# Row-shaped products with 512 moving weight columns, and a result stored in two halves

## Chip, cores and metric

The kernel runs on one core of one Trainium2 chip. The metric is the device time of one execution in microseconds (us). Before the change three runs took 415.16, 415.17 and 415.35 us, median 415.17. The profile is of one more execution.

## What is computed

One decode step for one token: a normalised row times wq gives 32 query heads; grouped attention over 4 key and value heads with 65,536 positions each; output projection; then a feed-forward block with gelu. x has 1024 elements, everything is bf16.

```
x  = A_x                                   # 1 x 1024
q  = layernorm(x) @ wq                     # 1024 x 4096, 32 heads of 128
o  = softmax(q k^T / sqrt(128)) v          # per group: 8 heads share 65536 x 128 of k and v
h  = x + o @ wo                            # 4096 x 1024
n  = layernorm(h)
h2 = h + (gelu(n @ w_gate) * (n @ w_up)) @ w_down    # 1024 x 3584, 1024 x 3584, 3584 x 1024
```

## The kernel before, in words

All weights and both caches are read once from HBM, 173 MB in all. SP issues every load, in program order, as transfers of up to 4 MB into one pool of four buffers (`chpool`): two for wq, 32 for K and V, two each for wo, gate, up and down. A load waits for the engine that still reads its buffer, and for one of eight completion semaphores: the ninth load after another waits for that one's landing. Each load has one packet for each of the 128 partitions, and they are spread evenly over 16 DMA engines.

Vectors of the token live as columns. Element `p * 8 + c` of x or h lies in partition `p`, column `c` (`x_col`, `h_col`); a matrix row with the same number is loaded to the same place (`"(p c) n -> p c n"`). LN1 and LN2 (`layernorm_cols`, L126) make `xn_bf` and `hn_bf` of them.

- q (L156 to L163): for each of 8 row groups `c` and 32 heads, a 128 x 128 block of wq is the stationary operand, and one column of `xn_bf` moves through it. The heads' 32 columns add up in `q_ps`.
- qsel and qs (L164 to L178): q is spread by selectors, then copied by POOL into zeroed tiles `qs`, one per group of heads (32 copies early on, 16 for each of two groups).
- K (L198): DVE transposes 128 x 1024 tiles into `kt` (a pool of six), PE multiplies with `qs`, DVE transposes scores back (L225) and takes maxima. The V pass of a group (L255) runs beside the K pass of the next one.
- wo (L297 to L335): `o2z` holds each of 32 columns of the attention result in a zeroed block of 32 columns, so that a product with 512 moving columns of wo writes 32 partitions, one of which is the result. Four column groups of the array (`tile_position`) take the 32 matrix rows in turn, `s` picks one of two PSUM banks. The four partial sums of each bank are copied out (L328 on DVE, L330 on ACT), and eight fp32 matmuls against a column of ones sum and turn them into columns, `hc_ps` (L333).
- Gate and up (`ffn_in`, L343): like q, but with 28 blocks per row group, whose columns are 28 apart (`f:F:FC`): 224 products each. Gate is loaded in two pieces, up in four (4, 2, 1 and 1 row groups). The gelu of gate is worked out in DVE and ACT beside up's products.
- Down (L380 to L398): 28 row groups with 8 blocks each (columns 8 apart), again one moving column, loaded in pieces of 10, 6, 4, 3, 2, 1, 1 and 1 row groups; the last of them goes in three parts of 8, 8 and 112 partitions.
- The residual is added at L402, and SP stores 16 bytes from each partition at L403.

The order on each engine is the program's, but for small pieces of work that the scheduler may move ahead.

Of the kernel before, what the change touches and what calls it, by code (L numbers as in the profile page):

```python
# [17 lines left out]
def kernel(  # L18
# [13 lines left out]
    nc = tc.nc  # L32
# [18 lines left out]
    DCH = 2  # L51
    CW = DCH * CH * Dh
    assert NCH % DCH == 0
    scale = float(Dh) ** -0.5
    eps = 1e-5
    assert Dh == P and rep * NS == SQ and NT % (CH * NH) == 0 and D % P == 0 and F % P == 0
# [69 lines left out]
    def layernorm_cols(src_col, dst_bf, tagp):  # L126
        s1 = small.tile([P, 1], F32, name=f"{tagp}_s1", tag="ln_s1")
        nc.vector.tensor_reduce(out=s1[:], in_=src_col, axis=AX.X, op=ALU.add)
        tot = misc([P, 1], F32, f"{tagp}_tot")
        nc.tensor.matmul(tot[:], lhsT=ones_f[:], rhs=s1[:], start=True, stop=True)  # L130
        mean = small.tile([P, 1], F32, name=f"{tagp}_mean", tag="ln_mean")
        nc.vector.tensor_scalar(out=mean[:], in0=tot[:], scalar1=1.0 / D, scalar2=None, op0=ALU.mult)
        xc = small.tile([P, DC], F32, name=f"{tagp}_xc", tag="ln_xc")
        nc.vector.tensor_scalar(out=xc[:], in0=src_col, scalar1=mean[:, 0:1], scalar2=None, op0=ALU.subtract)
        sq = small.tile([P, DC], F32, name=f"{tagp}_sq", tag="ln_sq")
        s2 = small.tile([P, 1], F32, name=f"{tagp}_s2", tag="ln_s2")
        nc.vector.tensor_tensor(out=sq[:], in0=xc[:], in1=xc[:], op=ALU.mult)
# [7 lines left out]
        nc.vector.tensor_scalar(out=dst_bf, in0=xc[:], scalar1=rstd[:, 0:1], scalar2=None, op0=ALU.mult)  # L145
# [168 lines left out]
    NW = D // 512  # L314
    at_ps = [misc([P, 512], F32, "at_ps") for _ in range(NW)]
    for w0 in range(0, Hq, WN):
        w_sb = chunk("wo_sb")
        wv = w_sb[:, 0:WN * D].rearrange("p (c n) -> p c n", c=WN)
        nc.sync.dma_start(out=wv, in_=wo_v[:, w0:w0 + WN, :])
        for cc in range(WN):  # L320
            c = w0 + cc
            q = c % 4
            for s in range(NW):
                nc.tensor.matmul(at_ps[s][32 * q:32 * q + 32, :], lhsT=o2z[:, c, :],  # L324
                                 rhs=wv[:, cc, s * 512:(s + 1) * 512],
                                 start=(c < 4), stop=(c >= Hq - 4), tile_position=(0, 32 * q))
    at_r = ktpool.tile([P, D], F32, name="at_r", tag="kt")
    nc.vector.tensor_copy(out=at_r[:, 0:512], in_=at_ps[0][:])  # L328
    for s in range(1, NW):
        nc.scalar.copy(out=at_r[:, s * 512:(s + 1) * 512], in_=at_ps[s][:])  # L330
# [7 lines left out]
    hn_bf = const.tile([P, DC], BF16, name="hn_bf")  # L338
    layernorm_cols(h_col[:], hn_bf[:], "ln2")
    GB = max(1, CW // F)  # L340
    assert DC % GB == 0

    def ffn_in(wmat, name, pieces):  # L343
        ps = misc([P, FC], F32, name)
        nc.vector.memset(ps[:], 0.0)
        wv_all = wmat.rearrange("(p c) n -> p c n", p=P)
        assert sum(pieces) == DC
        for c0 in range(0, DC, GB):
            w_sb = chunk("wgu_sb")
            wv = w_sb[:, 0:GB * F].rearrange("p (c n) -> p c n", c=GB)  # L350
            r0 = 0
            while r0 < GB:
                sz = pieces.pop(0)
                nc.sync.dma_start(out=wv[:, r0:r0 + sz, :], in_=wv_all[:, c0 + r0:c0 + r0 + sz, :])
                for cc in range(r0, r0 + sz):
                    for f in range(FC):
                        nc.tensor.matmul(ps[:, f:f + 1], lhsT=wv[:, cc, f:F:FC], rhs=hn_bf[:, c0 + cc:c0 + cc + 1],  # L357
                                         start=False, stop=False, skip_group_check=True)
# [17 lines left out]
    act_bf = const.tile([P, FC], BF16, name="act_bf")  # L376
    nc.vector.tensor_tensor(out=act_bf[:], in0=u_ps[:], in1=gl[:], op=ALU.mult)  # L377


    wd_v = B_w_down.rearrange("(p c) n -> p c n", p=P)  # L380
    DN = CW // D
    pieces = [[10, 6], [4, 3, 2, 1, 1, 1]]
    assert sum(map(sum, pieces)) == FC and max(map(sum, pieces)) <= DN
    d_ps = misc([P, DC], F32, "d_ps")
    nc.vector.memset(d_ps[:], 0.0)
    c0 = 0
    for group in pieces:
        w_sb = chunk("wd_sb")
        r0 = 0
        for sz in group:  # L390
            wv = w_sb[:, r0 * D:(r0 + sz) * D].rearrange("p (c n) -> p c n", c=sz)
            last = c0 + sz == FC
            for lo, hi in ((0, 8), (8, 16), (16, P)) if last else ((0, P),):
                nc.sync.dma_start(out=wv[lo:hi], in_=wd_v[lo:hi, c0:c0 + sz, :])
            for cc in range(sz):
                for j in range(DC):
                    nc.tensor.matmul(d_ps[:, j:j + 1], lhsT=wv[:, cc, j:D:DC], rhs=act_bf[:, c0 + cc:c0 + cc + 1],  # L397
                                     start=False, stop=False, skip_group_check=True)  # L398
# [3 lines left out]
    nc.vector.tensor_tensor(out=h2[:], in0=d_ps[:], in1=h_col[:], op=ALU.add)  # L402
    nc.sync.dma_start(out=out[0, 0].rearrange("(p c) -> p c", p=P), in_=h2[:])  # L403


# [28 lines left out]
```

## Time and profile before

| | us |
|---|---|
| the profiled execution | 414.91 |
| its span, first to last instruction | 413.1 |
| median of three other runs | 415.17 |
| PE busy (matmuls) | 256.8 |
| DVE busy | 201.9 |
| ACT busy | 35.9 |
| POOL busy | 27.1 |
| bytes moved | 173.33 MB, 420 GB/s over the span |
| q products, L160 (256) | 7.2 |
| gate products, L357 (224) | 14.3 |
| up products, L357 (224) | 14.3 |
| down products, L397 (224) | 13.6 |
| wo products, L324 (64) | 6.9 |
| fold of wo's result, L333 (16 passes) | 3.9 |

PE is the tensor engine's matmuls and PEld its weight loads, which overlap; DVE, ACT and POOL are the vector, scalar and general engines; SP issues DMAs. The page's slices cut the span in 40 equal parts, and each digit is the busy share in tenths; PEclk is the tensor clock as granted. In a timeline, a line has the start, the length, engine, line of the kernel, operation, tiles, shapes and count, and in brackets how long the engine idled and for whom. An "xN" after a busy time is a number of instructions. An fp32 matmul shows as two passes.

### The profile page before, as it was taken

To read this page: it belongs to the slowest core of one execution; us is meant where nothing else is said; L and a number is where in the kernel's file an instruction comes from. 1 tells how busy PE (TensorE), PEld (TensorE's weight loads), DVE (VectorE), ACT (ScalarE), POOL (GpSimd) and SP (SyncE) were. 2 spreads that over 40 slices of the span, in tenths; PEclk is the share of its full clock that TensorE was granted. 3 is DMA by queue.
4 is the path that set the end of the run, shared out by engine and by line. 5 is a ranking of instruction groups with operands and counts; after the bars stand their busy time and mean duration, and the time that the engine had idled before them with its cause. 6 is when DMAs were issued, how large, how long until landed. Compare 5 with 4: busy or idle time off the path is not lost.

```text
span 413.1 us, 4925 instructions
## 1 busy us (share of the span) xinstructions
PE 256.8 (62%) x2117; PEld 138.3 (33%) x2117; DVE 201.9 (49%) x254; ACT 35.9 (9%) x135; POOL 27.1 (7%) x100
## 2 busy tenths in 40 slices
PE   1336677698291838765566388191928335479997
PEld 1332222243130314221222233030314113279997
DVE  3107999999393808856474389291910000010000
ACT  1000000070000080000003400000071000000000
POOL 8123000310000210000000000000000000000000
PEclk9999989989886867895959698777796755655555
DMA  8999999999999999999999999999999999999993
GB/s 356 420 439 432 428 435 424 431 431 427 435 428 435 427 432 428 430 431 431 424 435 428 435 428 433 428 435 427 431 431 427 435 428 436 423 431 414 425 409 115
DMA packets 7413, 173.33 MB, mean 420 GB/s; under 512 B 992, under 2 KB 992, under 8 KB 1888
## 3 DMA queue, kind: packets, MB, share of 16 engines
q1 hardware_dynamic: 7360, 173.02, 98.0%
q8 instruction: 16, 0.26, 0.3%
q14 instruction: 5, 0.04, 0.0%
q10 hardware_dynamic: 32, 0.00, 0.0%
HBM read 173.02 MB, written 0.00 MB: 419 GB/s over the span
## 4 chain that ended last, share of the span: by engine, by line
DMA 52%; DVE 23%; PE 15%; issue 9%; SPq 0%; POOLq 0%; ACT 0%; POOL 0%; ACTq 0%
DMA k_sb<-in_A_k_cache_dram 44%; DVE kt L211 19%; DMA v_sb<-in_A_v_cache_dram 8%; PE g_ps L357 3%; PE u_ps L357 3%; PE d_ps L397 3%; PE qk_ps L215 2%; DVE mx L226 2%; DVE sc L225 2%; PE acc_ps L264 1%; PE o_ps L278 0%; SPq L87 0%; POOLq L429 0%; ACT acc_sb L275 0%; PE mxT_ps L233 0%
## 5 line engine op out<-in xcount | busy, mean ns | idle before, releaser
L215 PE MATMUL qk_ps<-kt,qs 128*128 128x512 bf16 x512 | 143.7, 436 | 78.8 <-DVE kt L211 76.7
L211 DVE STREAM_TRANSPOSE kt<-k_sb 128x1024 f32<-128x1024 f32 x128 | 146.2, 1208 | 53.5 <-DMA k_sb<-in_A_k_cache_dram 53.5
L215 PEld LDWEIGHTS <-qs 128*128 128x128 bf16 x512 | 54.9, 107 | 164.5 <-issue 120.9
L248 ACT ACTIVATE pt<-sc,nbias 128x256 bf16<-128x256 f32 x64 | 31.5, 492 | 275.2 <-DVE nbias L241 275.2
L264 PE MATMUL acc_ps<-v_sb,pt 128*32 128x512 bf16 x512 | 38.0, 444 | 13.5 <-DMA v_sb<-in_A_v_cache_dram 13.5
L357 PEld LDWEIGHTS <-wgu_sb 128*128 128x128 bf16 x448 | 28.5, 172 | 1.3 <-issue 1.3
L280 DVE TENSOR_TENSOR oT_all<-o_ps,rl 128x8 bf16<-128x8 f32 x4 | 0.7, 167 | 55.1 <-PE o_ps L278 55.1
L264 PEld LDWEIGHTS <-pt 128*32 128x32 bf16 x512 | 13.9, 107 | 33.0 <-issue 25.2
L225 DVE STREAM_TRANSPOSE sc<-qk_ps 128x512 f32<-128x512 f32 x32 | 22.1, 692 | 2.1 <-PE qk_ps L215 2.1
L226 DVE TENSOR_REDUCE mx<-sc 128x8 f32<-128x512 f32 x32 | 22.0, 688 | 1.1
L278 PE MATMUL o_ps<-sel,acc_sb 128*128 128x8 f32 x32 | 7.5, 364 | 21.8 <-ACT acc_sb L275 21.8
L357 PE MATMUL g_ps<-hn_bf,wgu_sb 128*128 128x1 bf16 x224 | 14.3, 202 | 1.2 <-DVE hn_bf L145 1.2
L278 PEld LDWEIGHTS o_ps<-sel,acc_sb 128*128 128x128 f32 x32 | 7.1, 328 | 23.0 <-ACT acc_sb L275 23.0
L357 PE MATMUL u_ps<-hn_bf,wgu_sb 128*128 128x1 bf16 x224 | 14.3, 202 | 0.0
L173 POOL MEMSET qs<- 128x2048 bf16 x4 | 7.2, 1803 | 102.6 <-PE qk_ps L215 102.6
L160 PE MATMUL q_ps<-xn_bf,wq_sb 128*128 128x1 bf16 x256 | 7.2, 165 | 10.8 <-DMA wq_sb<-in_A_wq_dram 10.8
L397 PE MATMUL d_ps<-act_bf,wd_sb 128*128 128x1 bf16 x224 | 13.6, 198 | 0.3 <-DVE act_bf L377 0.3
L397 PEld LDWEIGHTS <-wd_sb 128*128 128x128 bf16 x224 | 13.6, 164 | 0.2 <-issue 0.2
L177 POOL COPY qs<-qsel 32x32 bf16<-32x32 bf16 x64 | 11.2, 247 | 17.1 <-DVE qsel L168 16.4
L324 PE MATMUL at_ps<-wo_sb,o2z 128*32 128x512 bf16 x64 | 6.9, 609 | 8.5 <-DMA wo_sb<-in_A_wo_dram 8.5
L248 ACT ACTIVATION_READ_ACCUMULATOR pt<-sc,nbias 128x1 f32 x64 | 11.9, 186 | 0.0
L312 POOL MEMSET o2z<- 128x1024 bf16 x1 | 0.9, 950 | 156.6 <-PE acc_ps L264 156.6
(80 smaller groups left out, 61.3 us busy)
## 6 DMA issues: line engine op xcount, KB each, us to landing
k_sb<-in_A_k_cache_dram SPq DMA_DIRECT2D x16, 4096.0 KB, 29.8
v_sb<-in_A_v_cache_dram SPq DMA_DIRECT2D x16, 4096.0 KB, 33.1
wq_sb<-in_A_wq_dram SPq DMA_DIRECT2D x2, 4096.0 KB, 12.1
wo_sb<-in_A_wo_dram SPq DMA_DIRECT2D x2, 4096.0 KB, 36.5
wgu_sb<-in_B_w_gate_dram SPq DMA_DIRECT2D x2, 3584.0 KB, 33.4
wgu_sb<-in_B_w_up_dram SPq DMA_DIRECT2D x1, 3584.0 KB, 31.6
wd_sb<-in_B_w_down_dram SPq DMA_DIRECT2D x1, 2560.0 KB
wgu_sb<-in_B_w_up_dram SPq DMA_DIRECT2D x1, 1792.0 KB, 26.4
```

The source lines that it names most:

```text
L160: nc.tensor.matmul(q_ps[:, h:h + 1], lhsT=wq_tiles[c][:, h * P:(h + 1) * P], rhs=xn_bf[:, c:c + 1], start=False, stop=False, skip_group_ch ...
L173: nc.gpsimd.memset(qs[:], 0.0)
L177: nc.gpsimd.tensor_copy(out=qs[rows, :, s, SQ * i + s:SQ * (i + 1):NS], in_=qsel[rows, :, g * rep:(g + 1) * rep])
L211: nc.vector.transpose(out=kt[:], in_=k32[:, s * W:(s + 1) * W])
L215: nc.tensor.matmul(qk[:], lhsT=st["qs"][:, jt, s, :], rhs=mv[:, :, J, :, t], start=(s == 0 and jt == 0), stop=(s == NS - 1 and jt == 3))
L225: nc.vector.transpose(out=sc.rearrange("p n h s -> p (n h s)"), in_=qk[:])
L226: nc.vector.tensor_reduce(out=st["mx"][:, :, ci], in_=sc.rearrange("p n h s -> p h n s"), axis=AX.XY, op=ALU.max)
L248: nc.scalar.activation(out=pt[:].rearrange("p c n h s -> p (c n) h s")[:, :, r, :], in_=sc[:].rearrange("p c n h s -> p (c n) h s")[:, :, ...
L264: nc.tensor.matmul(acc[32 * c:32 * c + 32, :], lhsT=pt[:, ci % CPH, n, :, :].rearrange("p h s -> p (h s)"), rhs=v_sb[:, n:CH:NN, :], start ...
L278: nc.tensor.matmul(o_ps[:], lhsT=acc_sb[:, t * Dh:(t + 1) * Dh], rhs=sel[:, t:SQ:NS], start=(t == 0), stop=(t == NS - 1))
L357: nc.tensor.matmul(ps[:, f:f + 1], lhsT=wv[:, cc, f:F:FC], rhs=hn_bf[:, c0 + cc:c0 + cc + 1], start=False, stop=False, skip_group_check=True)
L397: nc.tensor.matmul(d_ps[:, j:j + 1], lhsT=wv[:, cc, j:D:DC], rhs=act_bf[:, c0 + cc:c0 + cc + 1], start=False, stop=False, skip_group_check ...
```

## The change

Vectors are now laid out in blocks of 512: element `t * 512 + p * 4 + c` lies in partition `p`, column `t * 4 + c`, and x, all weight rows and the result follow it (`"(t p c) n -> t p c n"` with c = 4). Products of q, of gate, of six of up's eight row groups and of 16 of down's 28 take the form that wo had: the vector's column, in a zeroed block of 32 (`xz`, `actz`), is stationary, and 512 weight columns move. Each row of weights spreads its blocks of 512 over the four column groups and, with more than four blocks, over two PSUM banks. What they sum is copied out and turned into columns by fp32 matmuls against selectors (`sel4`, `sel2`). The last two row groups of up and the last twelve of down keep one moving column; their 128 stationary columns are now 4 elements apart. wo's partial sums share one bank (two column groups for each half of a row), and four matmuls fold them in place of eight. Down is loaded in pieces of 4, 4, 4, 4, 4, 4, 2, 1 and 1 row groups. The result is stored in two halves of 8 bytes a partition, one issued by SP and one by ACT. `xz` is used again for LN2's result; wide sums take the PSUM buffers of the scores (`ps_qk`).

```diff
-    x_in = const.tile([XU, XV, DC], BF16, name="x_in")
-    nc.scalar.dma_start(out=x_in[:], in_=A_x[0, 0].rearrange("(u v c) -> u v c", u=XU, v=XV))
+    x_in = const.tile([XU, DS, XV, C4], BF16, name="x_in")
+    nc.scalar.dma_start(out=x_in[:], in_=A_x[0, 0].rearrange("(t u v c) -> u t v c", t=DS, u=XU, v=XV))
...
+    sel4 = const.tile([P, 4], F32, name="sel4")
+    nc.vector.tensor_copy(out=sel4[:], in_=ident_f[:, 0:P:32])
+    sel2 = const.tile([P, 2], F32, name="sel2")
+    nc.vector.tensor_tensor(out=sel2[:], in0=sel4[:, 0:2], in1=sel4[:, 2:4], op=ALU.add)
...
-    xn_bf = const.tile([P, DC], BF16, name="xn_bf")
-    layernorm_cols(x_col[:], xn_bf[:], "ln1")
+    xz = const.tile([P, DC, 32], BF16, name="xz")
+    nc.gpsimd.memset(xz[:], 0.0)
+    layernorm_cols(x_col[:], xz[:, :, 0], "ln1")
+
+    def wide_rows(banks, rows_z, ci, w_row, first, last):
+        for t in range(w_row.shape[-1] // NB):
+            q = t % 4
+            nc.tensor.matmul(banks[t // 4][32 * q:32 * q + 32, :], lhsT=rows_z[:, ci, :],
+                             rhs=w_row[:, t * NB:(t + 1) * NB], start=first, stop=last, tile_position=(0, 32 * q))
+
+    def evacuate(banks, nt, name):
+        r = ktpool.tile([P, len(banks), NB], F32, name=name, tag="kt")
+        for b, ps in enumerate(banks):
+            kp = 32 * min(4, nt - 4 * b)
+            if b == 0:
+                nc.vector.tensor_copy(out=r[0:kp, b, :], in_=ps[0:kp, :])
+            else:
+                nc.scalar.copy(out=r[0:kp, b, :], in_=ps[0:kp, :])
+        return r
+
+    def to_columns(dst, r, nt):
+        for b in range(r.shape[1]):
+            nq = min(4, nt - 4 * b)
+            for c in range(C4):
+                nc.tensor.matmul(dst[:, 16 * b + c:16 * b + 4 * nq:C4], lhsT=r[0:32 * nq, b, c:NB:C4],
+                                 rhs=sel4[0:32 * nq, 0:nq], start=False, stop=False, skip_group_check=True)
...
-    for c in range(DC):
-        for h in range(Hq):
-            nc.tensor.matmul(q_ps[:, h:h + 1], lhsT=wq_tiles[c][:, h * P:(h + 1) * P], rhs=xn_bf[:, c:c + 1],
-                             start=False, stop=False, skip_group_check=True)
+            wide_rows(q_banks, xz, ci, wq_tiles[t][:, cc, :], ci == 0, ci == DC - 1)
+    q_r = evacuate(q_banks, HD // NB, "q_r")
+    for b in range(2):
+        for hh in range(4):
+            nc.tensor.matmul(q_ps[:, 16 * b + hh:16 * b + 16:4], lhsT=q_r[:, b, hh * P:(hh + 1) * P], rhs=sel4[:],
+                             start=True, stop=True)
...
-            q = c % 4
-            for s in range(NW):
-                nc.tensor.matmul(at_ps[s][32 * q:32 * q + 32, :], lhsT=o2z[:, c, :],
+            for s in range(DS):
+                q = 2 * (c % 2) + s
+                nc.tensor.matmul(at_ps[32 * q:32 * q + 32, :], lhsT=o2z[:, c, :], rhs=wv[:, cc, s * NB:(s + 1) * NB],
...
+    def fold_columns(dst, ps, name):
+        r = ktpool.tile([P, NB], F32, name=name, tag="kt")
+        nc.scalar.copy(out=r[:], in_=ps[:])
+        for c in range(C4):
+            nc.tensor.matmul(dst[:, c:DC:C4], lhsT=r[:, c:NB:C4], rhs=sel2[:], start=False, stop=False,
+                             skip_group_check=True)
...
                 for cc in range(r0, r0 + sz):
-                    for f in range(FC):
-                        nc.tensor.matmul(ps[:, f:f + 1], lhsT=wv[:, cc, f:F:FC], rhs=hn_bf[:, c0 + cc:c0 + cc + 1],
+                    ci = t * C4 + cc
+                    if ci < n_wide:
+                        wide_rows(banks, hz, ci, wv[:, cc, :], ci == 0, ci == n_wide - 1)
+                        if ci == n_wide - 1:
+                            to_columns(ps, evacuate(banks, FT, name + "_r"), FT)
+                    else:
+                        for f in range(FC):
+                            k, c = divmod(f, C4)
+                            nc.tensor.matmul(ps[:, f:f + 1], lhsT=wv[:, cc, k * NB + c:(k + 1) * NB:C4], rhs=hz[:, ci, 0:1],
...
-    g_ps = ffn_in(B_w_gate, "g_ps", [4, 4])
+    g_ps = ffn_in(B_w_gate, "g_ps", [4, 4], DC)
...
-    u_ps = ffn_in(B_w_up, "u_ps", [4, 2, 1, 1])
+    actz = ptpool.tile([P, FC, 32], BF16, name="actz", tag="pt")
+    nc.gpsimd.memset(actz[:], 0.0)
+    u_ps = ffn_in(B_w_up, "u_ps", [4, 2, 1, 1], DC - 2)
...
+        if t < TW:
+            nc.sync.dma_start(out=wv, in_=wd_v[t])
+            for cc in range(C4):
+                for s in range(DS):
+                    q = 2 * (cc % 2) + s
+                    nc.tensor.matmul(dw_ps[32 * q:32 * q + 32, :], lhsT=actz[:, t * C4 + cc, :],
+                                     rhs=wv[:, cc, s * NB:(s + 1) * NB], start=(t == 0 and cc < 2),
+            if t == TW - 1:
+                fold_columns(d_ps, dw_ps, "dw_r")
+            continue
...
+        for sz in (2, 1, 1) if t == FT - 1 else (C4,):
+            nc.sync.dma_start(out=wv[:, r0:r0 + sz, :], in_=wd_v[t][:, r0:r0 + sz, :])
+            for cc in range(r0, r0 + sz):
                 for j in range(DC):
-                    nc.tensor.matmul(d_ps[:, j:j + 1], lhsT=wv[:, cc, j:D:DC], rhs=act_bf[:, c0 + cc:c0 + cc + 1],
+                    k, c = divmod(j, C4)
+                    nc.tensor.matmul(d_ps[:, j:j + 1], lhsT=wv[:, cc, k * NB + c:(k + 1) * NB:C4],
+                                     rhs=actz[:, t * C4 + cc, 0:1], start=False, stop=False, skip_group_check=True)
...
-    nc.sync.dma_start(out=out[0, 0].rearrange("(p c) -> p c", p=P), in_=h2[:])
+    for t in range(DS):
+        (nc.sync if t % 2 == 0 else nc.scalar).dma_start(out=out_v[t], in_=h2[:, t * C4:(t + 1) * C4])
```

Here DS = 2, C4 = 4, NB = 512, FT = 7 and TW = 4. In the changed kernel `wide_rows` stands at L173, `to_columns` at L194, `fold_columns` at L377, the narrow products of up at L412, down's wide ones at L452 and its narrow ones at L464.

More of the change, by code (lines that the diff above doesn't have):

```diff
@@ L53 @@
     assert NCH % DCH == 0
+    NB = 512
+    C4 = NB // P
+    DS = D // NB
+    FT = F // NB
     scale = float(Dh) ** -0.5
     eps = 1e-5
-    assert Dh == P and rep * NS == SQ and NT % (CH * NH) == 0 and D % P == 0 and F % P == 0
+    assert Dh == P and rep * NS == SQ and NT % (CH * NH) == 0 and D % NB == 0 and F % NB == 0 and C4 == 4
     const = ctx.enter_context(tc.tile_pool(name="const", bufs=1))
@@ L73, in misc @@
         return ps_m.tile(shape, dtype, name=name, tag="misc")
-    wq_v = A_wq.rearrange("(p c) n -> p c n", p=P)
-    WB = CW // HD
-    assert WB >= 1 and DC % WB == 0
+    wq_v = A_wq.rearrange("(t p c) n -> t p c n", p=P, c=C4)
+    assert C4 * HD == CW
     XU = 16
     XV = P // XU
-    x_in = const.tile([XU, XV, DC], BF16, name="x_in")
-    nc.scalar.dma_start(out=x_in[:], in_=A_x[0, 0].rearrange("(u v c) -> u v c", u=XU, v=XV))
+    x_in = const.tile([XU, DS, XV, C4], BF16, name="x_in")
+    nc.scalar.dma_start(out=x_in[:], in_=A_x[0, 0].rearrange("(t u v c) -> u t v c", t=DS, u=XU, v=XV))
     wq_tiles = []
-    for c0 in range(0, DC, WB):
+    for t in range(DS):
         w_sb = chunk("wq_sb")
-        wv = w_sb[:, 0:WB * HD].rearrange("p (c n) -> p c n", c=WB)
-        nc.sync.dma_start(out=wv, in_=wq_v[:, c0:c0 + WB, :])
-        wq_tiles.extend(wv[:, i, :] for i in range(WB))
+        wv = w_sb[:].rearrange("p (c n) -> p c n", c=C4)
+        nc.sync.dma_start(out=wv, in_=wq_v[t])
+        wq_tiles.append(wv)
     ones_f = const.tile([P, P], F32, name="ones_f")
@@ L149 @@
     for v in range(XV):
-        nc.tensor.matmul(x_ps[:], lhsT=xsel[:, v, :], rhs=x_in[:, v, :], start=(v == 0), stop=(v == XV - 1))
+        nc.tensor.matmul(x_ps[:].rearrange("p (t c) -> p t c", t=DS), lhsT=xsel[:, v, :], rhs=x_in[:, :, v, :],
+                         start=(v == 0), stop=(v == XV - 1))
     x_col = const.tile([P, DC], F32, name="x_col")
     nc.vector.tensor_copy(out=x_col[:], in_=x_ps[:])
-    xn_bf = const.tile([P, DC], BF16, name="xn_bf")
-    layernorm_cols(x_col[:], xn_bf[:], "ln1")
@@ L156 @@
-    q_ps = misc([P, Hq], F32, "q_ps")
-    nc.vector.memset(q_ps[:], 0.0)
-    for c in range(DC):
-        for h in range(Hq):
-            nc.tensor.matmul(q_ps[:, h:h + 1], lhsT=wq_tiles[c][:, h * P:(h + 1) * P], rhs=xn_bf[:, c:c + 1],
-                             start=False, stop=False, skip_group_check=True)
+    xz = const.tile([P, DC, 32], BF16, name="xz")
[6 more added lines that the diff above has]
+                             rhs=w_row[:, t * NB:(t + 1) * NB], start=first, stop=last, tile_position=(0, 32 * q))
@@ new lines, in bank_pair @@
+    def bank_pair(name, n=2):
+        return [ps_qk.tile([P, NB], F32, name=name, tag="qk") for _ in range(n)]
+    def evacuate(banks, nt, name):
[7 more added lines that the diff above has]
+        return r
@@ new lines, in to_columns @@
+    def to_columns(dst, r, nt):
[4 more added lines that the diff above has]
+                                 rhs=sel4[0:32 * nq, 0:nq], start=False, stop=False, skip_group_check=True)
+    q_banks = bank_pair("qw_ps")
+    for t in range(DS):
+        for cc in range(C4):
+            ci = t * C4 + cc
+            wide_rows(q_banks, xz, ci, wq_tiles[t][:, cc, :], ci == 0, ci == DC - 1)
@@ L313 @@
     nc.gpsimd.tensor_copy(out=o2z[:, :, 0], in_=o2_bf[:])
-    NW = D // 512
-    at_ps = [misc([P, 512], F32, "at_ps") for _ in range(NW)]
+    at_ps = bank_pair("at_ps", 1)[0]
     for w0 in range(0, Hq, WN):
@@ L321 @@
             c = w0 + cc
-            q = c % 4
-            for s in range(NW):
[L324 to L330, printed above, removed]
+            for s in range(DS):
+                q = 2 * (c % 2) + s
+                nc.tensor.matmul(at_ps[32 * q:32 * q + 32, :], lhsT=o2z[:, c, :], rhs=wv[:, cc, s * NB:(s + 1) * NB],
+                                 start=(c < 2), stop=(c >= Hq - 2), tile_position=(0, 32 * q))
@@ L331 @@
+    def fold_columns(dst, ps, name):
[4 more added lines that the diff above has]
+                             skip_group_check=True)
     hc_ps = misc([P, DC], F32, "hc_ps")
-    for j in range(DC):
-        nc.tensor.matmul(hc_ps[:, j:j + 1], lhsT=at_r[:, j:D:DC], rhs=ones_f[:, 0:1], start=True, stop=True)
+    nc.vector.memset(hc_ps[:], 0.0)
@@ L334, with ffn_in @@
+    fold_columns(hc_ps, at_ps, "at_r")
     h_col = const.tile([P, DC], F32, name="h_col")
     nc.vector.tensor_tensor(out=h_col[:], in0=hc_ps[:], in1=x_col[:], op=ALU.add)
[L338 to L343, printed above, removed]
+    hz = xz
+    layernorm_cols(h_col[:], hz[:, :, 0], "ln2")
+    assert C4 * F <= CW
+    def ffn_in(wmat, name, pieces, n_wide):
         ps = misc([P, FC], F32, name)
@@ L345, in ffn_in @@
         nc.vector.memset(ps[:], 0.0)
-        wv_all = wmat.rearrange("(p c) n -> p c n", p=P)
-        assert sum(pieces) == DC
-        for c0 in range(0, DC, GB):
+        banks = bank_pair(name + "_w")
+        wv_all = wmat.rearrange("(t p c) n -> t p c n", p=P, c=C4)
+        for t in range(DS):
             w_sb = chunk("wgu_sb")
-            wv = w_sb[:, 0:GB * F].rearrange("p (c n) -> p c n", c=GB)
+            wv = w_sb[:, 0:C4 * F].rearrange("p (c n) -> p c n", c=C4)
             r0 = 0
-            while r0 < GB:
+            while r0 < C4:
@@ L353, in ffn_in @@
                 sz = pieces.pop(0)
-                nc.sync.dma_start(out=wv[:, r0:r0 + sz, :], in_=wv_all[:, c0 + r0:c0 + r0 + sz, :])
+                nc.sync.dma_start(out=wv[:, r0:r0 + sz, :], in_=wv_all[t][:, r0:r0 + sz, :])
                 for cc in range(r0, r0 + sz):
-                    for f in range(FC):
-                        nc.tensor.matmul(ps[:, f:f + 1], lhsT=wv[:, cc, f:F:FC], rhs=hn_bf[:, c0 + cc:c0 + cc + 1],
-                                         start=False, stop=False, skip_group_check=True)
+                    ci = t * C4 + cc
+                    if ci < n_wide:
[6 more added lines that the diff above has]
+                            nc.tensor.matmul(ps[:, f:f + 1], lhsT=wv[:, cc, k * NB + c:(k + 1) * NB:C4], rhs=hz[:, ci, 0:1],
+                                             start=False, stop=False, skip_group_check=True)
@@ L374 @@
     nc.vector.scalar_tensor_tensor(out=gl[:], in0=th[:], scalar=1.0, in1=hg[:], op0=ALU.add, op1=ALU.mult)
-    u_ps = ffn_in(B_w_up, "u_ps", [4, 2, 1, 1])
[L376 to L383, printed above, removed]
+    actz = ptpool.tile([P, FC, 32], BF16, name="actz", tag="pt")
@@ L384 @@
+    nc.gpsimd.memset(actz[:], 0.0)
+    u_ps = ffn_in(B_w_up, "u_ps", [4, 2, 1, 1], DC - 2)
+    nc.vector.tensor_tensor(out=actz[:, :, 0], in0=u_ps[:], in1=gl[:], op=ALU.mult)
+    wd_v = B_w_down.rearrange("(t p c) n -> t p c n", p=P, c=C4)
+    DN = CW // (C4 * D)
+    TW = min(DN, FT - 1)
     d_ps = misc([P, DC], F32, "d_ps")
     nc.vector.memset(d_ps[:], 0.0)
-    c0 = 0
-    for group in pieces:
-        w_sb = chunk("wd_sb")
-        r0 = 0
[L390 to L395, printed above, removed]
+    dw_ps = bank_pair("dw_ps", 1)[0]
@@ new lines @@
+    for t in range(FT):
+        if t % DN == 0:
+            w_sb = chunk("wd_sb")
+        o = (t % DN) * C4 * D
+        wv = w_sb[:, o:o + C4 * D].rearrange("p (c n) -> p c n", c=C4)
+        if t < TW:
+            nc.sync.dma_start(out=wv, in_=wd_v[t])
+            for cc in range(C4):
+                for s in range(DS):
+                    q = 2 * (cc % 2) + s
+                    nc.tensor.matmul(dw_ps[32 * q:32 * q + 32, :], lhsT=actz[:, t * C4 + cc, :],
+                                     rhs=wv[:, cc, s * NB:(s + 1) * NB], start=(t == 0 and cc < 2),
+                                     stop=(t == TW - 1 and cc >= C4 - 2), tile_position=(0, 32 * q))
+            if t == TW - 1:
+                fold_columns(d_ps, dw_ps, "dw_r")
+            continue
+        r0 = 0
+        for sz in (2, 1, 1) if t == FT - 1 else (C4,):
+            nc.sync.dma_start(out=wv[:, r0:r0 + sz, :], in_=wd_v[t][:, r0:r0 + sz, :])
+            for cc in range(r0, r0 + sz):
@@ L396 @@
                 for j in range(DC):
-                    nc.tensor.matmul(d_ps[:, j:j + 1], lhsT=wv[:, cc, j:D:DC], rhs=act_bf[:, c0 + cc:c0 + cc + 1],
-                                     start=False, stop=False, skip_group_check=True)
-            c0 += sz
+                    k, c = divmod(j, C4)
+                    nc.tensor.matmul(d_ps[:, j:j + 1], lhsT=wv[:, cc, k * NB + c:(k + 1) * NB:C4],
+                                     rhs=actz[:, t * C4 + cc, 0:1], start=False, stop=False, skip_group_check=True)
@@ L402 @@
     nc.vector.tensor_tensor(out=h2[:], in0=d_ps[:], in1=h_col[:], op=ALU.add)
-    nc.sync.dma_start(out=out[0, 0].rearrange("(p c) -> p c", p=P), in_=h2[:])
+    out_v = out[0, 0].rearrange("(t p c) -> t p c", p=P, c=C4)
+    for t in range(DS):
+        (nc.sync if t % 2 == 0 else nc.scalar).dma_start(out=out_v[t], in_=h2[:, t * C4:(t + 1) * C4])
 _INS = ['A_x', 'A_k_cache', 'A_v_cache', 'A_wq', 'A_wo', 'B_x', 'B_w_gate', 'B_w_up', 'B_w_down']
```

## Prediction

> **What bounds the kernel now.** I read the page's slices first, then the stretches of the tail, then its timeline.
>
> ```profile
> PE   1336677698291838765566388191928335479997
> PEclk9999989989886867895959698777796755655555
> DMA  8999999999999999999999999999999999999993
> ```
>
> The DMA engines are full from the second slice to the last but one: 173 MB at some 430 GB/s. Only what lies after the last byte can be won, and whatever keeps that byte late must not get worse. PE is full in the last slices, at half clock. The stretches there (columns: from:to, length, busy us of PE, PEld, DVE, ACT, POOL, clock, DMA share, GB/s):
>
> ```profile
> 393.00:400.00 7.00, 6.72 (x110) 6.78 (x110) 0.19 (x1) 0.00 (x0) 0.00 (x0) 0.50 0.98 408
> 400.00:403.90 3.90, 3.90 (x68) 3.90 (x68) 0.00 (x0) 0.00 (x0) 0.00 (x0) 0.50 1.00 401
> 405.20:408.00 2.80, 2.80 (x50) 2.80 (x49) 0.00 (x0) 0.00 (x0) 0.00 (x0) 0.50 0.48 169
> 408.00:411.00 3.00, 2.49 (x42) 2.40 (x41) 0.17 (x1) 0.00 (x0) 0.00 (x0) 0.50 0.00 0
> ```
>
> The transfers thin out at 404 us and stop at 408 (some of the 16 engines run about 3.5 us behind others; the last semaphore update of a weight load is at 408.44), but PE works until 410.5. The timeline says on what:
>
> ```profile
> 368.13 14.33 PE L357 MATMUL g_ps<-hn_bf,wgu_sb 128*128 128x1 bf16 x224 [1.24 <-DVE hn_bf L145]
> ...
> 382.32 14.33 PE L357 MATMUL u_ps<-hn_bf,wgu_sb 128*128 128x1 bf16 x224
> ...
> 396.92 13.57 PE L397 MATMUL d_ps<-act_bf,wd_sb 128*128 128x1 bf16 x224 [0.28 <-DVE act_bf L377]
> ...
> 410.53 0.17 DVE L402 TENSOR_TENSOR h<-d_ps,h_col 128x8 bf16<-128x8 f32 x1 [13.66 <-PE d_ps L397]
> 410.72 0.38 SPq L403 DMA_DIRECT2D out_dram<-h  x1
> ```
>
> Gate, up and down are one unbroken PE run of 42.4 us, 672 one-column products at 64, 64 and 60.6 ns (14.33/224, 13.57/224). No transfer ends it. The add starts 2.1 us after the last landing; from there to the end (413.1) it is 2.57 us.
>
> **The change, part by part.**
>
> *Wide products.* A row of weights (one `ci`) costs 7 matmuls of 512 columns instead of 28 narrow ones. The nearest row is the output projection, which is already of this kind (32-column weights, 512 moving, four column groups):
>
> ```profile
> 356.13 3.33 PE L324 MATMUL at_ps<-wo_sb,o2z 128*32 128x512 bf16 x32 [6.12 <-DMA wo_sb<-in_A_wo_dram]
> ```
>
> 32 in 3.33 us, 0.104 each; four start together every 0.43 us. Seven take two such rounds, 0.85 us a row, against 28 x 64 ns = 1.79. Gate: 8 rows, 6.8 us instead of 14.3.
>
> *Folding back into columns.* It is added behind each wide sum: a copy out of PSUM (0.69 us on DVE at L328, 0.58 on ACT at L330, side by side) and fp32 matmuls with 128x128 weights, two passes each; L333 has 16 passes in 3.93 us, 0.245 each. The gate, up and q folds have 8 matmuls, 3.9 us; the one of down (and of `at`) has 4, 2.0 us.
>
> *Narrow products that stay.* Two rows of up (56) and 12 of down (96) keep one moving column, but their weights lie 4 elements (8 bytes) apart rather than 28 or 8. No row has that step. The ends: q's packed weights (L160, 128 in 3.57 us) 27.9 ns, and down's step of 16 bytes, 60.6. Is q at the same clock? The page gives full clock before 38 us, but I don't believe it:
>
> ```profile
> 36.26 0.14 PEld L215 LDWEIGHTS <-qs 128*128 128x128 bf16 x1 [0.28 <-issue]
> 36.69 0.14 PEld L215 LDWEIGHTS <-qs 128*128 128x128 bf16 x1 [0.28 <-issue]
> ...
> 38.30 1.62 PEld L215 LDWEIGHTS <-qs 128*128 128x128 bf16 x8 [0.18 <-issue]
> ```
>
> The same matmuls are 0.43 us apart before 38.3 and 0.20 after, so the clock rose only then, and q ran at half clock like the tail. The step, not the clock, makes 28 into 61. Since 16 bytes and 56 bytes differ by only 5%, the penalty has saturated at 16, and 8 lies between: by a straight line from 2 to 16 bytes 42 ns. I take 42; it will turn out that anything below 45 gives the same time.
>
> On this the Trainium skill has a rule ("SBUF — State Buffer", Door 1: The DMA port swizzle): lines of 16 bytes, full speed if each is hit at least twice. That fits the two rows and would make 8 bytes cost 28 ns; the sum stays as it is. But the same note calls a step of 8 bf16 free, and this is the 60.6 ns row: there the trace decides.
>
> *The front.* Before, q was ready 3.6 us after its second tile's landing (24.0). Now it is 3.4 (32 wide at half clock) + 0.75 copies + 3.9 fold, and qsel comes at 33.0 instead of 28.5, the first 16 copies of L177 (0.18 each) at 36.0 instead of 31.5. The first QK matmul was at 35.0; it moves by 1 us. Six kt buffers let the transposes from 33.7 on run ahead, and the loads in flight cover the rest: a 4 MB chunk moves in 9.7 us and the tightest K load (issued at 90.84) lands 20.6 us later, so some 10 us are spare. The wq buffers come free as early as before (32 x 0.104 against 128 x 0.028). Cost 0; without that cover 1 us. `xz`'s memset on POOL, the two selectors on DVE and the finer pieces of x_in lie ahead of wq's landing at 12.9: 0.
>
> *Output projection and second norm.* Four fold matmuls for eight save 2 us (362.1 against 364.3 for h_col), so hz is ready at 365.9. That gains nothing by itself: what follows waits for weights. Second halves land (semaphore updates of before) at 373.1 for gate, 381.6 and 385.9, 388.1, 390.3 for up.
>
> *Now the tail's chain*, with these landings. Gate: 365.9 + 3.4; second half 373.1 + 3.4 = 376.5, copies, fold: 381.2. Up: 381.6 + 3.4; the two rows of 385.9 are done at 387.7, copies 388.5, fold 392.4, 56 narrow ones 394.8 (395.9 at 61 ns), multiply: actz at 395.1. Its memset on POOL waits for a score buffer free since half of the last V pass, and ends long before.
>
> Down: wd has the same bytes in pieces of 4,4,4,4,4,4,2,1,1 rows. By packets of before (8 KB 313 ns, 20 KB 765, 12 KB 464; eight per engine), 16 rows take 10.0 us instead of 9.8, so the fourth piece lands at 400.46 (was 400.27); then 402.96, 405.47, 406.8, 407.5, 408.2. As the late stretch of before ran slow for 1.3 us (403.9 to 405.2), the upper end of the last landing is 408.6. SP issues all of it earlier than now, because gate's buffers come free at 369 and 376.5 instead of 375.4 and 382.5; eight loads are in flight at most in both, and the queue is never short.
>
> PE from 400.46: 8 wide 0.95 = 401.4, ACT copy 402.0, four fold matmuls 404.05 (the narrow ones queue behind them on PE, so this wait counts), 32 narrow x 42 = 405.4. The next piece lands at 405.47: from here PE waits for DMA. 32 more: 406.9; 16: 407.6; 8: 407.9; the last 8 after 408.25: 408.6, and 0.15 for the last one's end: add at **408.75** (409.15 with the late landing) against 410.53. Below 45 ns it is the same; at 60.6 PE is behind throughout: 404.05 + 96 x 0.0606 = 409.87, add at 410.0.
>
> *Store.* The halves go out on SP and ACT together (issue 0.38 and 0.41), each 128 elements of 8 bytes; before, 128 of 16 bytes took 0.2 us of packets. Between -0.1 (fewer bytes a packet) and +0.3 (a second queue's packets, one more wait at the end); I take +0.1. The skill ("DMA: Bandwidth & Descriptors", Issuing engines are not separate DMA queues) says that a second issuing engine saves only issue time; by it the half on ACT hides its own issue and no more, sum unchanged.
>
> **Sum**: -1.78 + 0.1 = -1.7, with the late landing -1.3; I take -1.6. Against the profiled execution (span 413.1, time 414.91) 413.3; the median of the runs is 415.17, 0.26 above it, so 413.6.
>
> **Rivals.**
> A: *narrow products stay at 61 ns*, PE remains the bound: -0.53 + 0.1, 414.7. For: the saturated step cost. Against: 8 bytes is nearer to packed than to saturated.
> B: *wide products overlap two ways, not four*, since seven column groups in two banks alternate unevenly: slower. From 365.9 PE then has 130 wide ones, three folds with copies (11.9) and 152 narrow ones (6.4), plus 0.5 of small steps: 384.7 + 130w. It equals today's 410.5 at w = 0.2 us; at 0.213 it ends at 412.4, time 417.2. Against: the 0.104 of L324, whose order of groups was no better.
> C: *the new layout of wq, gate, up and down streams worse* (30.5 MB, 71 us). From 2.2% on (1.6 us) nothing is won; 4% (2.8 us) gives 416.4. Against: packets of 28 to 32 KB keep their size, 8 KB ones cost 3% in 17 us alone, which is in the sum.
> D: *the lagging engines lag less*, because PE has 2931 instead of 4089 instructions to fetch, and the fetches (16 of 16 KB on the instruction queue) delay single engines by 1.5 us: another -1, 412.6.
>
> **Numbers.** Forecast 413.6: 0.54; A 0.25; B 0.08; C 0.08; D 0.05. A run can tell about 0.2% (0.8 us) from no change. Faster: 0.9 of the forecast, D, a fifth of A: 0.59. Same: the rest of the forecast, three quarters of A, a little of C: 0.26. Slower: B, most of C, the end of A: 0.15. The range runs from just under D's 412.6 to 415.6, which is A's 414.7 with 0.9 for a late landing (0.4), a dear store (0.2) and the spread of runs (0.2); B and most of C are left out.
>
> **What would show it.** L464's 96 products as short bursts with DMA waits between them, and the add 0.3 to 0.6 us after the last landing (right); one solid PE run of 5.8 us after the fold (A); L173 groups of four more than 0.43 us apart (B); GB/s below 425 where wq or gate streams, or a last landing past 409 (C). If actz came after 397, the up chain would be the miss, and the wide part of down would no longer wait for weights.

## The result and the profile after

The changed kernel takes 414.37 us (median of 12 runs, 414.05 to 414.72) against 415.24 (12 runs) before: a ratio of 0.9978, 95% interval 0.9969 to 0.9987. It is 0.87 us faster, where 1.6 were forecast. The profiled execution took 414.39 with a span of 412.6; before it was 414.91 with 413.1.

The slices of the changed kernel's page still show a full DMA to the end, and a PE that is no longer full in the tail:

```profile
PE   1375777698491838665566388192828335457855
PEclk9999889969886877895959688777775555667655
DMA  8999999999999999999999999999999999999992
```

The same stretches of the tail as before (busy us of PE, PEld, DVE, ACT, POOL, then clock, DMA share, GB/s):

```profile
393.00:400.00 7.00, 3.46 (x34) 1.09 (x33) 0.28 (x1) 0.00 (x0) 0.00 (x0) 0.50 1.01 419
400.00:403.90 3.90, 3.09 (x22) 2.19 (x21) 0.00 (x0) 0.59 (x1) 0.00 (x0) 0.50 0.99 402
405.20:408.00 2.80, 2.58 (x64) 2.36 (x64) 0.00 (x0) 0.00 (x0) 0.00 (x0) 0.50 0.16 58
408.00:411.00 3.00, 0.03 (x1) 0.00 (x0) 0.17 (x1) 0.00 (x0) 0.00 (x0) 0.50 0.05 1
```

In 393 to 400 PE is half idle, and after 408 it has nothing left: the 2.5 us of products that came after the last byte are gone. The changed kernel's timeline shows what PE waits for now:

```profile
372.99 3.31 PE L173 MATMUL g_ps_w<-wgu_sb,xz 128*32 128x512 bf16 x28 [3.76 <-DMA wgu_sb<-in_B_w_gate_dram]
...
381.50 3.60 PE L173 MATMUL u_ps_w<-wgu_sb,xz 128*32 128x512 bf16 x28 [0.72 <-DMA wgu_sb<-in_B_w_up_dram]
...
391.32 2.00 PE L412 MATMUL u_ps<-xz,wgu_sb 128*128 128x1 bf16 x56
...
401.85 2.03 PE L377 MATMUL d_ps<-sel,dw_r 128*128 128x2 f32 x8 [0.69 <-ACT dw_r L375]
...
403.74 1.19 PE L464 MATMUL d_ps<-actz,wd_sb 128*128 128x1 bf16 x32
...
407.60 0.43 PE L464 MATMUL d_ps<-actz,wd_sb 128*128 128x1 bf16 x8 [0.22 <-DMA wd_sb<-in_B_w_down_dram]
408.06 0.17 DVE L468 TENSOR_TENSOR h<-d_ps,h_col 128x8 bf16<-128x8 f32 x1 [14.43 <-PE d_ps L464]
```

In brackets are transfers now. The last eight products start 0.05 us after the last landing (407.55), and the add comes at 408.06, 2.47 us earlier than before. But the span shrank by 0.5 only. The missing 1.95 us lie behind the add: from it to the end it is 4.55 us, where it was 2.60 (from the traces' own ends, 412.61 and 413.13). The list of DMA issues (KB, then us from issue to landing) names the place. Before:

```profile
out_dram<-h SPq DMA_DIRECT2D x1, 2.0 KB, 1.4
```

After:

```profile
out_dram<-h SPq DMA_DIRECT2D x1, 1.0 KB, 3.2
out_dram<-h ACTq DMA_DIRECT2D x1, 1.0 KB, 3.3
```

Half the bytes take more than twice as long to land. The packets themselves are through at 409.35, 0.25 us after the first; the semaphore updates that tell of them trickle in from 409.57 to 411.58. Before, the packets of 16 bytes ended at 411.78 and the updates came from 411.99 to 412.17.

### The profile page after: what moved, and what is told of

Read it like the earlier page. It is cut to its first block, busy times and chain, and to the rows that moved or that the text cites. A ratio compares the mean times of both kernels' runs of the same rounds, so it can differ in the third digit from the quotient of the medians.

```text
span 412.6 us, 3869 instructions
## 1 busy us (share of the span) xinstructions
PE 248.1 (60%) x1583; PEld 113.7 (28%) x1583; DVE 203.2 (49%) x258; ACT 38.3 (9%) x139; POOL 28.2 (7%) x102
## 4 chain that ended last, share of the span: by engine, by line
DMA 61%; DVE 21%; issue 9%; PE 8%; SPq 0%; POOLq 0%; ACT 0%; POOL 0%; ACTq 0%
DMA k_sb<-in_A_k_cache_dram 43%; DVE kt L257 17%; DMA wd_sb<-in_B_w_down_dram 9%; DMA v_sb<-in_A_v_cache_dram 8%; PE qk_ps L261 5%; DVE mx L272 2%; DVE sc L271 2%; PE acc_ps L310 1%; PE g_ps_w L173 1%; PE o_ps L324 0%; PE bc_ps L285 0%; SPq L92 0%; POOLq L497 0%; ACT acc_sb L321 0%; PE mxT_ps L279 0%
## 5 line engine op out<-in xcount | busy, mean ns | idle before, releaser
L261 PE MATMUL qk_ps<-kt,qs 128*128 128x512 bf16 x512 | 145.6, 443 | 74.4 <-DVE kt L257 72.7
L310 PE MATMUL acc_ps<-v_sb,pt 128*32 128x512 bf16 x512 | 36.8, 435 | 14.0 <-DMA v_sb<-in_A_v_cache_dram 14.0
L173 PEld LDWEIGHTS <-xz 128*32 128x32 bf16 x162 | 6.9, 134 | 25.5 <-issue 21.4
L173 PE MATMUL qw_ps<-wq_sb,xz 128*32 128x512 bf16 x64 | 7.2, 629 | 9.0 <-DMA wq_sb<-in_A_wq_dram 9.0
L173 PE MATMUL g_ps_w<-wgu_sb,xz 128*32 128x512 bf16 x56 | 6.9, 609 | 4.9 <-DMA wgu_sb<-in_B_w_gate_dram 3.8
```

What stands on the lines that cost most here:

```text
L173: nc.tensor.matmul(banks[t // 4][32 * q:32 * q + 32, :], lhsT=rows_z[:, ci, :], rhs=w_row[:, t * NB:(t + 1) * NB], start=first, stop=last, ...
L261: nc.tensor.matmul(qk[:], lhsT=st["qs"][:, jt, s, :], rhs=mv[:, :, J, :, t], start=(s == 0 and jt == 0), stop=(s == NS - 1 and jt == 3))
L310: nc.tensor.matmul(acc[32 * c:32 * c + 32, :], lhsT=pt[:, ci % CPH, n, :, :].rearrange("p h s -> p (h s)"), rhs=v_sb[:, n:CH:NN, :], start ...
```

## The experiments

My theory after the result: the tail's gain comes from the 8-byte step of the stationary columns, and the store in 8-byte pieces gives most of it back. The rivals: two issuers or the block layout make the store dear, not the size of its pieces; and the wide products make the gain in the tail, not the step.

**One store from SP, still 8-byte pieces.**

```diff
-    for t in range(DS):
-        (nc.sync if t % 2 == 0 else nc.scalar).dma_start(out=out_v[t], in_=h2[:, t * C4:(t + 1) * C4])
+    nc.sync.dma_start(out=out[0, 0].rearrange("(t p c) -> p t c", p=P, c=C4),
+                      in_=h2[:].rearrange("p (t c) -> p t c", c=C4))
```

> The changed kernel, with its result stored by one DMA from SP (still 8-byte pieces, two for each partition). In the changed kernel the two halves were issued at 408.26 and their last semaphore update came at 411.58, 3.3 us later, where the old single store of 16-byte pieces took 1.45 us. Theory P (pieces of 8 bytes are slow to be acknowledged, whoever issues them): the last update again about 3.3 us after the issue, time as the changed kernel, 414.2 to 414.6. Theory Q (two issuing engines at once, or the ACT queue, are what costs): about 1.5 us after the issue, time about 412.6.

Measured: 414.06 us, ratio to before 0.9973 (0.9962 to 0.9984). The one DMA's issue and landing:

```profile
out_dram<-h SPq DMA_DIRECT2D x1, 2.0 KB, 3.1
```

The landing is as late with one issuer and one queue. Theory Q falls. The two halves are no better than one store: 0.3 us worse by the medians (0.2 when each is taken against its own runs of the kernel before), with intervals that overlap.

**The kernel before, its store in halves.** Only the last lines change; neighbouring partitions stay 16 bytes apart in memory.

```diff
-    nc.sync.dma_start(out=out[0, 0].rearrange("(p c) -> p c", p=P), in_=h2[:])
+    out_v = out[0, 0].rearrange("(p c) -> p c", p=P)
+    for t in range(2):
+        (nc.sync if t % 2 == 0 else nc.scalar).dma_start(out=out_v[:, 4 * t:4 * t + 4], in_=h2[:, 4 * t:4 * t + 4])
```

> The kernel before, with only its store changed: two halves of 8 bytes a partition, SP and ACT. All else, the layout too, is as before, and the add comes at 410.5. Theory P: the store takes about 1.8 us longer, time 417.0. Theory Q: the same 417.0. Theory R (it is the block layout, where the 8-byte pieces of neighbouring partitions follow each other in memory, and not the pieces' size): neighbours are here 16 bytes apart, the store takes 1.5 us as before, time 415.2.

Measured: 416.79 us, ratio 1.0037 (1.0024 to 1.0050). Its two stores:

```profile
out_dram<-h SPq DMA_DIRECT2D x1, 1.0 KB, 2.7
out_dram<-h ACTq DMA_DIRECT2D x1, 1.0 KB, 3.2
```

The store alone, without any other part of the change, costs 1.7 us, in the old layout too: theory R falls. What is left is the size of the pieces, or their number, which goes with it: the same 2 KB are 256 pieces of 8 bytes or 128 of 16.

**Back to 16-byte pieces.**

```diff
+    for t in range(DS):
+        for par in range(2):
+            nc.tensor.matmul(o_ps[64 * t:64 * t + 64, par * C4:(par + 1) * C4], lhsT=ident_bf[:, par:P:2],
+                             rhs=h2[:, t * C4:(t + 1) * C4], start=True, stop=True, tile_position=(0, 64 * t))
+    nc.vector.tensor_copy(out=ho[:], in_=o_ps[:])
+    nc.sync.dma_start(out=out[0, 0].rearrange("(p c) -> p c", p=P), in_=ho[:])
```

> The changed kernel, with four small bf16 matmuls against slices of the identity that bring the finished result back to 8 consecutive elements in a partition, one copy out of PSUM, and one store from SP in 16-byte pieces. Theory P and R: some 0.6 us are added ahead of the store (matmuls 0.3, copy 0.2, waits 0.1), and the store falls from 3.3 to 1.45 us: about 1.2 us faster than the changed kernel, 413.1. Theory that neither the size nor the layout matters but the lateness of the store in a quiet machine: no gain, 415.0.

Measured: 413.55 us, ratio 0.9961 (0.9947 to 0.9975). Its timeline from the add on:

```profile
408.53 0.17 DVE L468 TENSOR_TENSOR h<-d_ps,h_col 128x8 bf16<-128x8 f32 x1 [14.86 <-PE d_ps L464]
408.75 0.27 PE L472 MATMUL o_ps<-h,ident_bf 128*64 128x4 bf16 x4 [0.26 <-DVE h L468]
...
409.06 0.17 DVE L475 CAST ho<-o_ps 128x8 bf16<-128x8 f32 x1 [0.36 <-PE o_ps L472]
409.25 0.35 SPq L476 DMA_DIRECT2D out_dram<-ho  x1
```

The way back costs 0.52 us (issue 0.72 after the add instead of 0.20), and the store lands 1.4 us after its issue. That is 1.4 us won behind the add, where 1.2 were expected; 0.5 of it is lost because the stream itself ended 0.47 us later (last landing 408.02), so that the time is 413.55 and not 413.1. The theory of no gain (415.0) falls. The late end looks like one of this kernel, not of one execution: its five runs took 413.39 to 413.75, where the changed kernel's twelve less 1.4 us would give 412.65 to 413.32. Why the stream ends later here no run shows.

**32-byte pieces**, from 64 partitions, by eight matmuls instead of four (`lhsT=ident_bf[:, par:P:4]`, `P` becomes 64 in the store).

> As the run with four small matmuls and 16-byte pieces, but with eight matmuls to 64 partitions and pieces of 32 bytes. Theory P1 (8 bytes are below a limit, 16 above it): the store again lands 1.4 us after its issue, the four more matmuls add 0.1 to 0.2, time 413.6 to 413.8. Theory P2 (the cost goes on falling with the size of the pieces): the store lands after 1.1 us or less, time 413.4 or less.

Measured: 413.82 us, ratio 0.9968 (0.9955 to 0.9981), issue to landing 1.7 us, not the 1.4 of theory P1; 0.2 of it is a longer issue (0.55 us against 0.35). Larger pieces win nothing, so P2 falls, and of the three sizes only 8 bytes are dear. The number of pieces halves with each step (256, 128, 64), so these runs don't tell whether size or number sets the price.

**One moving column for all of gate, up and down.**

```diff
-                    if ci < n_wide:
-                        wide_rows(banks, hz, ci, wv[:, cc, :], ci == 0, ci == n_wide - 1)
...
+                    for f in range(FC):
...
-    TW = min(DN, FT - 1)
+    TW = 0
```

> The changed kernel, with all products of gate, up and down back to one moving column (no wide ones, no folds for them), in the new layout, in which the 128 stationary columns lie 8 bytes apart. q, wo and the store as changed. Theory S (the step of the stationary columns is what counts: 36 ns at 8 bytes in the changed kernel's trace against 61 to 64 at 16 and 56): a load's products (28 x 36 ns = 1.0 us a row of up, 8 x 36 = 0.29 a row of down) are done before the next load lands, the add comes 0.5 us after the last landing, and the time equals the changed kernel's, 414.2 to 414.6. Theory W (the wide products are needed): PE falls behind its weights, and the add comes over 1 us later, 415.4 or more.

Measured: 414.31 us, ratio 0.9979 (0.9970 to 0.9988), the changed kernel's own. Its timeline at the end:

```profile
400.09 1.23 PE L457 MATMUL d_ps<-actz,wd_sb 128*128 128x1 bf16 x32 [1.25 <-DMA wd_sb<-in_B_w_down_dram]
402.57 1.22 PE L457 MATMUL d_ps<-actz,wd_sb 128*128 128x1 bf16 x32 [1.25 <-DMA wd_sb<-in_B_w_down_dram]
...
408.03 0.17 DVE L461 TENSOR_TENSOR h<-d_ps,h_col 128x8 bf16<-128x8 f32 x1 [16.45 <-PE d_ps L457]
```

Each piece's 32 products take 1.2 us and wait 1.25 us for the next piece. The add comes at 408.03: theory W falls. The wide products, folds and selectors for gate, up and down are not needed; the block layout, which brings the steps of the stationary columns to 8 bytes, is enough. q and wo keep their wide products in this run, as in all that follow with the new layout.

**The step alone, undone.** Down's last twelve row groups take their stationary columns 16 bytes apart; their sums go to other columns of the result, the rest is the changed kernel.

```diff
-                    nc.tensor.matmul(d_ps[:, j:j + 1], lhsT=wv[:, cc, k * NB + c:(k + 1) * NB:C4],
+                    nc.tensor.matmul(d_ps[:, j:j + 1], lhsT=wv[:, cc, j:D:DC],
```

> The changed kernel; only the 96 one-column products of down's last twelve row groups take their 128 stationary columns 8 elements (16 bytes) apart in place of 4, so their sums go to other columns of the result. Theory S (the step sets the cost): 60.6 ns each as in the kernel before, against 36 to 37 in the changed kernel; PE works without a pause from the end of the fold (403.9) for 5.8 us, the add comes at 409.7 and not 408.06, time about 416.0. Theory C (the clock or the neighbourhood of the wide products made them faster, not the step): 36 ns again, 414.4.

Measured: 415.71 us, ratio 1.0013 (1.0004 to 1.0023): slower than before. In its timeline the products form one unbroken run:

```profile
403.66 5.91 PE L464 MATMUL d_ps<-actz,wd_sb 128*128 128x1 bf16 x96
409.60 0.17 DVE L468 TENSOR_TENSOR h<-d_ps,h_col 128x8 bf16<-128x8 f32 x1 [15.85 <-PE d_ps L464]
```

5.91/96 is 61.6 ns, at the same place, clock and moving operand at which the changed kernel needs 37.2 (1.19/32). The end of the last product weighs more in a short run; from start to start it is 60 ns against 33. Theory S holds, and 96 products' step is worth 1.54 us of the add's time.

**The pieces of the last loads.** The kernel before, with down's pieces as after.

```diff
-    pieces = [[10, 6], [4, 3, 2, 1, 1, 1]]
+    pieces = [[4, 4, 4, 4], [4, 4, 2, 1, 1]]
...
-            for lo, hi in ((0, 8), (8, 16), (16, P)) if last else ((0, P),):
+            for lo, hi in ((0, P),):
```

> The kernel before, with down loaded in the pieces of the changed one (4, 4, 4, 4, 4, 4, 2, 1, 1 row groups) and the last row group in one DMA instead of three. The last landing was at 408.44 before and at 407.55 in the changed kernel. Theory L (the small pieces at the end, whose packets slowed at 404 to 405 us, cost it): 407.5 to 407.9 here. Theory M (the block layout, or a faster stream as a whole): 408.3 or later. PE ends the kernel in both cases, so the time stays at 415.1.

Measured: 415.15 us, ratio 0.9997 (0.9986 to 1.0007); the last landing is at 407.96. That lies between the two theories' numbers: 0.48 earlier than before, 0.41 later than in the changed kernel. The kernels after the change that share its loads landed at 407.48 to 408.06, so this difference is no larger than that between kernels with the same loads, and I don't count it as shown.

**Old order for the result.** Block layout for x, q, gate and up; gate, up and down with one moving column, gate and up at the 8-byte step (q stays wide); but down's columns, the residual and the output in the old order:

```diff
-                    nc.tensor.matmul(d_ps[:, j:j + 1], lhsT=wv[:, cc, k * NB + c:(k + 1) * NB:C4],
+                    nc.tensor.matmul(d_ps[:, j:j + 1], lhsT=wv[:, cc, j:D:DC],
...
+            nc.tensor.matmul(hr_ps[64 * t:64 * t + 64, par * C4:(par + 1) * C4], lhsT=ident_f[:, par:P:2],
+                             rhs=h_col[:, t * C4:(t + 1) * C4], start=True, stop=True, tile_position=(0, 64 * t))
...
+    nc.vector.tensor_tensor(out=h2[:], in0=d_ps[:], in1=h_row[:], op=ALU.add)
+    nc.sync.dma_start(out=out[0, 0].rearrange("(p c) -> p c", p=P), in_=h2[:])
```

> What the runs point to: the block layout for x, q, gate and up with one-column products alone, 8 bytes apart; down's result columns, the residual and the result in the old order, so that the store has 16-byte pieces and one issuer (four small fp32 matmuls behind gate bring the residual to the old order, in PE's idle time). Down's products then have a step of 16 bytes, 61 ns: 32 of them are 1.95 us, less than the 2.5 us between two landings, 8 are 0.49. The add comes 0.65 to 0.7 us after the last landing instead of 0.5, and the store takes 1.45 us instead of 3.3: with the last landing at 407.55 a span of 410.8 and a time of 412.6; 413.0 if the stream ends as late as in the run with the 16-byte pieces. If PE were the bound, the add would come over 1 us after the last landing.

Measured: 413.73 us, ratio 0.9963 (0.9950 to 0.9976). A miss by 0.7 to 1.1 us. Its timeline:

```profile
402.70 2.10 PE L464 MATMUL d_ps<-actz,wd_sb 128*128 128x1 bf16 x32 [0.38 <-DMA wd_sb<-in_B_w_down_dram]
405.20 4.03 PE L464 MATMUL d_ps<-actz,wd_sb 128*128 128x1 bf16 x64 [0.39 <-DMA wd_sb<-in_B_w_down_dram]
409.26 0.17 DVE L468 TENSOR_TENSOR h<-d_ps,h_row 128x8 bf16<-128x8 f32 x1 [17.57 <-PE d_ps L464]
```

I had compared rates (0.49 us of products for 0.62 of loading) and forgotten that a piece of four starts only when all of it has landed, 1.2 us before the piece of two. The last 64 products run through, and the add comes 1.54 us after the last landing (407.72). So the last eight row groups were loaded in smaller pieces:

```diff
-        for sz in (2, 1, 1) if t == FT - 1 else (C4,):
+        for sz in {FT - 1: (1, 1, 1, 1), FT - 2: (2, 1, 1)}.get(t, (C4,)):
```

> As the run with down's result, residual and output in the old order (down's step 16 bytes, 61 ns a product), which ended with PE 1.5 us behind the last landing; only down's last eight row groups are loaded as 2, 1, 1, 1, 1, 1, 1 instead of 4, 2, 1, 1. One row group is 0.49 us of products and 0.65 us of loading. If PE lagged there for the size of the piece of four alone (1.95 us of products that start only when all of it has landed, 1.2 us before the next piece): the add comes 0.65 to 0.75 us after the last landing, the small pieces add 0.2 us to the stream, time 413.0 to 413.3. If PE lags for another reason, the add stays 1.2 us or more behind and the time at 413.7.

Measured: 413.06 us, ratio 0.9948 (0.9934 to 0.9961), the fastest of all kernels here. The add is at 408.83, 0.83 us after the last landing (408.00): a little later than expected, and the lag was mainly that of the piece of four. It is not gone:

```profile
402.85 5.94 PE L464 MATMUL d_ps<-actz,wd_sb 128*128 128x1 bf16 x96 [0.42 <-DMA wd_sb<-in_B_w_down_dram]
```

The last 96 products still run through without a wait. They begin with the last piece of four, landed at 402.81, and PE catches up only near the end, so the add here hangs on PE and not on the last landing.

**Step and store together, no wide products** (the edits of the third and the fifth experiment).

> The two parts that the runs found to matter, and no wide products for gate, up and down: the block layout with one-column products 8 bytes apart (as in the run that had these alone, 414.31) and the small matmuls with the 16-byte store (which took 0.8 us off the changed kernel). If the two are independent: 413.5, with the last landing anywhere from 407.5 to 408.0, the add 0.5 us after it and the store issued 0.7 us after the add. If the wide products were worth anything beside the store: 414.0 or more.

Measured: 413.53 us, ratio 0.9961 (0.9949 to 0.9974), last landing 408.06: independent, as expected.

## Why the prediction was right, and what was off in it

The time lies in the range and the direction was right; the size was half of the forecast (0.87 of 1.6 us). There is luck in it: 414.37 lies nearer to rival A's 414.7 than to the forecast's 413.6, and the range reached so far up for A's sake, whose mechanism did not occur. The forecast's mechanism did occur in the tail, and two errors of opposite sign partly cancelled. By its steps:

- *What bounds it*: right. PE's run of gate, up and down ended the kernel, and only what lay behind the last landing could be won.
- *Wide products*: 28 took 3.3 to 3.6 us (forecast 3.4), four ways at once. Rival B fell with this line. The 14 of up's last wide piece took 1.17, not 1.7 (the granted clock was 0.87 in 385.8 to 387.0, where the forecast had half), and `actz` was ready at 393.6 instead of 395.1, which only lengthened a wait for weights.
- *Folds*: 3.89 and 2.03 us, against 3.9 and 2.0.
- *Step of 8 bytes*: 36 to 37 ns in the changed kernel's runs of 32 and 56, taken 42. Below the 45 from which it mattered, so without effect; the step undone brings PE's bound back, which is rival A's mechanism. The rule of the Trainium skill ("SBUF — State Buffer", Door 1: The DMA port swizzle) that a 16-byte line must be hit at least twice holds nearly, at 36 ns instead of the packed 28; its remark that a step of 8 bf16 is free does not hold for stationary columns: 61.6 ns.
- *Front*: the first QK products began at 35.31 instead of 35.02, and no load was late for it. Cost 0, as said, but with help: the second wq tile landed at 22.70 instead of 23.97, so the longer chain behind it (q at 30.5 instead of 27.8) moved less than forecast.
- *Last landing*: 407.55 where 408.2 (up to 408.6) was forecast, and the add 408.06 where 408.75 was. The fourth piece landed at 400.08 instead of 400.46, which I had worked out from the one trace of before, and the pieces behind it took 7.47 us instead of 7.74. That one trace did not fix the stream's end to better than 0.5 us: the four profiled kernels with these loads and an 8-byte store ended at 407.48 to 407.55, the four with larger pieces at 407.72 to 408.06, and no run shows why. Rival C fell.
- *Rival D* (fewer instruction fetches) isn't the cause: with the products all narrow, 15 fetches, against 12 in the changed kernel, left the last landing at 407.52.
- **The step that failed is the store**, "I take +0.1", between -0.1 and +0.3. It cost 1.95 us in the profiled pair, and 1.7 us by itself in the old kernel. I had taken the packets' 0.2 us for the price and not the wait for their acknowledgement; the row of before, 16-byte pieces, gave no bound for smaller ones. Had the term been right, the same sum with the tail's 2.47 us would have given a span of 410.7.

So the sum came out at 0.5 us in the profiled pair and 0.87 by the medians: a gain in the tail 0.7 us larger than forecast and a loss at the store 1.9 us larger. The skill's sentence on issuers ("DMA: Bandwidth & Descriptors", Issuing engines are not separate DMA queues) agrees with the first experiment: one issuer or two made no clear difference.

## What to carry to other kernels

A kernel that is bound by its stream to the last byte can, with the stream as it is, only be shortened behind that byte: look for the engine that still works there, for the size of the piece it waits for, and then for the store that ends it. Before rewriting products, look at the step of their stationary columns: a layout that brings it from 56 and 16 bytes to 8 did here what the wide form of gate, up and down was written for. The layout that made the step smaller also made the pieces of the result smaller, and the last store has nothing that hides it.

## What was not expected of the hardware

- A store of 2 KB in 8-byte pieces is acknowledged (last semaphore update) 2.7 to 3.3 us after its issue, in 16-byte pieces 1.4, in 32-byte pieces 1.7 (the issue itself 0.2 longer), although the packets are through within 0.25 us in all. The number of pieces changes with their size in all runs. What happens between packet and acknowledgement no trace here shows.
- Stationary columns of bf16 at steps of 2, 8, 16 and 56 bytes took 27.9, 36 to 37, 61 and 64 ns for one moving column at half clock; from start to start 27, 33, 60 and 63.
- The 16 semaphore updates of one load are up to 3.6 us apart at the end of the changed kernel, and up to 4.15 at the end of the one before. The large steps in this spread fall on fetches of instructions, 16 KB each: with the first of them at 19.64 us, the spread of the second wq tile's landing in the kernel before was 1.97 us, of the first tile's 0.58; in the changed kernel the first fetch comes at 31.89, the second wq tile's spread is 0.63 and that of the next load 2.20. Not every fetch adds to it.
- The granted clock on the page reads 1.00 before its first record (38.18 us in the kernel before). The 512-column products there started 0.43 us apart, and 0.22 apart behind it, so they ran at half clock.
